# A recurrent attention and gated feed-forward kernel: state products in attention's tiling, and a new plan of the instruction order

## The chip, the cores and the metric

The kernel runs on one core of one Trainium2 chip. The metric is the device time of one execution in microseconds; the time of a kernel is the median of its runs. Five engines work side by side: TensorE (PE; its weight loads are shown as PEld), VectorE (DVE), ScalarE (ACT), GpSimd (POOL) and SyncE (SP), which here issues the DMAs.

## The reference

Three stages follow one another on a batch of 4, 8 heads, 768 tokens, 48 values a head, in float32. `_attn_ref` is a linear recurrence with decay w and a bonus u for the current token; its output, 384 wide, goes into a gated layer with a product over the tokens, and that into a convolution gate.

```python
def _attn_ref(r, k, v, w, u):
    for t in range(S):
        kt, vt, rt = (k[:, :, t], v[:, :, t], r[:, :, t])
        cur = np.einsum('bhd,bhe->bhde', u[None] * kt, vt)
        y[:, :, t] = np.einsum('bhd,bhde->bhe', rt, state + cur)
        state = w[None, :, :, None] * state + np.einsum('bhd,bhe->bhde', kt, vt)

def _moe_ref(x, w_in, w_spatial, b_spatial, w_out):
    h = np.maximum(x @ w_in, 0.0)
    u, v = (h[..., :d_ff // 2], h[..., d_ff // 2:])
    v_n = (v - mu) / np.sqrt(var + 1e-06)
    v_s = np.einsum('ts,bsd->btd', w_spatial, v_n) + b_spatial[None, :, None]
    return ((u * v_s) @ w_out)

def _moe2_ref(x, w_val, conv_w, w_out):
    for k in range(K):
        gate_pre += conv_w[k][None, None, :] * xp[:, k:k + S, :]
    gate = 1.0 / (1.0 + np.exp(-gate_pre))
    return (gate * (x @ w_val) @ w_out)
```

## The kernel before

**Attention in chunks.** A batch is cut into 6 chunks of 128 tokens; the 8 heads lie as 4 pairs, the two heads of a pair at partitions 0 and 64. For chunk i, `load_chunk` brings kT and rT (heads on partitions, two DMAs for rT) and tok (tokens on partitions: k, r, and v in blocks of 32). `prep_chunk` scales them on GpSimd with tables of powers of w, multiplies r, k and u for the bonus, and scales k for the state by the far table (`k_far`, tile tk3); VectorE sums the bonus and ScalarE spreads it on the diagonal of A (L522). `scores` (L545) makes 8 products of 48 rows, and VectorE copies what lies above the diagonal into A (L549). `attend` adds rT times the state S_bd (L573, chunks 1 to 5) and A times v (L577), all in tiles of 32 columns. `state_update` (L606) multiplies k by v into the bank P, 8 products of 48 columns, two column tiles of 64; VectorE scales S_bd by the decay (L612) and adds P (L619; L621 copies in a batch's first chunk). The last chunk of a batch has no state step, so there are 20 in all. All of these products are float32, and each leaves two MATMUL records in the trace.

**Feed-forward part.** float32 values are split into a high and a low part of a faster format, and a product is three MATMULs (`split3`, L632). In order: `value` (pv, 9 products of 512 columns, once a chunk), `gate_in` (pu), `spatial` (ps, L719), `proj` (pd), the convolution on VectorE (L767), `val` (pf), `out_mm` (pg, L804) and the store. The weights come as 64-bit floats; `split_f64` decodes them on ScalarE (L358) and VectorE (L360, L362, L364) and splits them (L401, L402). w_in has two halves of three slices of 512 KB: wv for `value` and wu for `gate_in`.

**The order.** No loop order is kept. Each step is an `op` of the class `Plan` with an engine, an assumed duration, its reads and writes and the buffers that it takes. `Plan.order` simulates the engines and, at each step, takes among the ops that can start earliest the one of highest level: the longest path to the end, plus a bias from the table `FAVOR` (by name, and by chunk, weight slice or stage: stages 0 to 3 are batch 0, 4 the middle batches, 5 the last). A PE op in the tiling of the op before it (`mode`) gets `STAY` more; one in another costs `SWITCH` more time. The modes are "" (full array), "r" (scores), "c" (attend) and "s" (state). Loads are issued by SyncE in that order; a load under 4 KB is assumed to land 1.7 us after its issue, a larger one to share 360 B/ns. The three feed-forward inputs that are single rows (u, and b_sp twice) are spread over the partitions by a TensorE product (L444) and copied by ScalarE (L447). In the planned gaps of the first 40 us, `warm` puts dummy products (L310) before the next op that takes a PSUM buffer.

Of the kernel before, what the change touches and what calls it, by code (L numbers as in the profile page):

```python
# [16 lines left out]
B, H, S, D = 4, 8, 768, 48  # L17
# [19 lines left out]

STAGES = 6
FAVOR = {
    ("attend", 4): 1761900, ("attend", 5): 649800,  # L40
    ("bonus_fill", 'c5'): -99500, ("bonus_fill", 3): -1684500, ("bonus_fill", 4): -306700, ("bonus_fill", 5): -2300,
    ("bonus_sum", 'c3'): -51200, ("bonus_sum", 4): -127800,
    ("bonus_u", 4): 42200, ("bonus_u", 5): -636500,
    ("conv_tap", 3): 230200, ("conv_tap", 4): 204100, ("conv_tap", 5): -665000,
    ("decode_shift", 'wu0'): -635700, ("decode_shift", 'wv2'): 524400,
    ("gate_in", 2): -390500,
    ("k_far", 3): 74400,
    ("k_scale", 3): -1024300,
    ("load_kT", 'c0'): 7800,
    ("load_rT", 'c0'): -340400, ("load_rT", 3): 141900, ("load_rT", 5): -610300,  # L50
    ("load_tok", 'c1'): -1066400, ("load_tok", 4): -17900,
    ("load_wu", 'w1'): 12100,
    ("load_wv", 'w1'): -1258600,
    ("norm_aggr", 'c4'): -134100,
    ("out_copy", 4): 204600,
    ("proj", 3): -35700, ("proj", 5): -12300,
    ("proj_low", 4): -188700,
    ("scores_keep", 4): 272400, ("scores_keep", 5): 278300,
    ("spatial", 4): 685200, ("spatial", 5): -5400,
    ("spatial_high", 3): 258700,  # L60
    ("state", 4): 703000,
    ("val", 3): -36600, ("val", 4): -172300, ("val", 5): -506100,
    ("val_gate", 3): 549700,
    ("val_low", 3): 627700,
    ("value", 4): 558600,
    ("value_relu", 4): 1075200,
    ("x_high", 4): -699900,
    ("x_low", 'c0'): 321000,
}


class Plan:
# [5 lines left out]

    AFTER = {"PE": 200, "ACT": 140, "DVE": 130, "POOL": 100, "SP": 10}
    EVAC = 4000  # L80
    SWITCH, STAY = 95, 408100
    COLD, RAMP = 6900, 40000
    FLOW = 4000
    FIRST = {"SP": 800, "DVE": 900, "ACT": 2150, "POOL": 1900, "PE": 1100}

    def __init__(self):
# [34 lines left out]
    def order(self, slots, free_tags):  # L121
        n = len(self.ops)
        after = lambda a, b: 0 if a == b == "PE" else self.AFTER[a]
        succ = [[] for _ in range(n)]
        for i, o in enumerate(self.ops):
            for p in o[3]:
                succ[p].append((i, after(self.ops[p][0], o[0])))
        left = [len(o[3]) for o in self.ops]
        level = [0.0] * n
        for i in range(n - 1, -1, -1):  # L130
            o = self.ops[i]
            d = o[1] + (2050 + o[6] / 360 if o[6] else 0)
            level[i] = d + max((level[j] + x for j, x in succ[i]), default=0)
        level = [x + o[5] for x, o in zip(level, self.ops)]
        ready = [0.0] * n
        avail = {}
        for i in range(n):
            if not left[i]:
                avail.setdefault(self.ops[i][0], set()).add(i)
        start, end, slot_free = [None] * n, [None] * n, [0.0] * n  # L140
        engine, dma_free, issue_free = dict(self.FIRST), self.FLOW, 0.0
        turn = {t: 0 for t in slots}
        uleft = {k: len(u) for k, u in self.users.items()}
        ufree = {k: 0.0 for k in self.users}
        free = {t: [0.0] * c for t, c in slots.items()}
        dual = {"DVE": (0.0, 0.0), "POOL": (0.0, 0.0)}
        other = {"DVE": "POOL", "POOL": "DVE"}
        mode = ""

        def slot_time(i):  # L150
            t, want = 0.0, {}
            for k in self.ops[i][4]:
                tag = self.tile_tag[k]
                q = want.get(tag, 0)
                want[tag] = q + 1
                if tag not in free_tags and self.tag_order[tag][turn[tag] + q] != k:
                    return None
                if len(free[tag]) <= q:
                    return None
                t = max(t, sorted(free[tag])[q])  # L160
            return t

        for _ in range(n):
            best, first = None, None
            for e, group in avail.items():
                seen = []
                for i in group:
                    t = max(ready[i], engine[e])
                    if self.ops[i][4]:
                        s = slot_time(i)  # L170
                        if s is None:
                            continue
                        t = max(t, s)
                    if self.ops[i][8]:
                        lo, hi = dual[other[e]]
                        if lo <= t < hi:
                            t = hi
                    seen.append((t, i))
                if seen:
                    t = min(seen)[0]  # L180
                    if first is None or t < first or (t == first and e == "POOL"):
                        first, best = t, (e, seen)
            if best is None:
                raise RuntimeError("no order")
            e, seen = best
            i = -max((level[i] + self.STAY * (e == "PE" and self.ops[i][9] == mode), -i)
                     for t, i in seen if t <= first)[1]
            t, o = first, self.ops[i]
            avail[e].discard(i)
            d = o[1]  # L190
            if e == "PE":
                d += self.SWITCH * (o[9] != mode)
                mode = o[9]
            if o[8]:
                dual[e] = (t, t + d)
            start[i], slot_free[i] = t, slot_time(i)
            engine[e] = t + d
            end[i] = t + d
            if o[6]:
                issue_free = max(issue_free, t) + 450 * o[7]  # L200
                if o[6] < 4096:
                    end[i] = issue_free + 1700
                else:
                    dma_free = max(dma_free, issue_free + 850) + o[6] / 360
                    end[i] = dma_free + 900
            for k in o[4]:
                tag = self.tile_tag[k]
                free[tag].remove(min(free[tag]))
                turn[tag] += 1
            for k in self.touch[i]:  # L210
                uleft[k] -= 1
                ufree[k] = max(ufree[k], end[i] + self.AFTER[e])
                if not uleft[k]:
                    free[self.tile_tag[k]].append(ufree[k])
            for j, x in succ[i]:
                ready[j] = max(ready[j], end[i] + x)
                left[j] -= 1
                if not left[j]:
                    avail.setdefault(self.ops[j][0], set()).add(j)
        self.start, self.end, self.slot_free = start, end, slot_free  # L220
        return sorted(range(n), key=lambda i: (start[i], i))

    def run(self, slots, free_tags, keep_clock=None):
# [6 lines left out]
        for i in self.order(slots, free_tags):  # L230
            if self.ops[i][0] == "PE" and keep_clock and self.start[i] < self.RAMP:
                busy = max(busy, self.slot_free[i] + 300)
                cold = max(0.0, min(self.start[i], self.COLD) - busy)
                keep_clock[0] = int(cold // 107 + max(0.0, self.start[i] - max(busy, self.COLD)) // 70)
                busy = self.end[i]
            self.ops[i][2]()
            if keep_clock:
                keep_clock[0] = 0
# [19 lines left out]
def rwkv_mlp_kernel(  # L258
# [59 lines left out]
    def op(*a, **k):  # L318
        plan.op(*a, **k)
# [273 lines left out]
    def state_update(i):  # L593
# [6 lines left out]
        def mm():  # L600
            make()
            k, v = st[tk], vals(i)
            for q in range(NP):
                for g in range(2):
                    h = 2 * q + g
                    nc.tensor.matmul(st[pk][64 * g:64 * g + D, q, :], k[:, D * h:D * h + D],  # L606
                                     v[:, q].rearrange("p (x c) -> p x c", c=Q)[:, g::2], start=True, stop=True)
        op("state", "PE", 520, mm, ((tk, "k"), (tk, "v")), ((pk,),), (pk,), mode="s")
        blocks = S_bd.rearrange("r p (x c) -> r p x c", c=Q)

        def scale():
# [123 lines left out]
    def proj(b, hf, m):  # L735
# [7 lines left out]
        def mm():  # L743
# [2 lines left out]
                for make in mk:  # L746
                    make()
            split3(st[pk], wo, [st[gh], st[gl]], 4, lambda w, kt: w[:, kt, C * m:C * m + C], lambda x, kt: x[:, kt, :])
        op("proj", "PE", ns_r(HALF, 12), mm, tuple((k, q) for k in (gh, gl) for q in range(4)) + wkeys("wo", 4), ((pk,),), (pk, xh, xl, gt) if m == 0 else (pk,))

        def hi():
            nc.scalar.copy(st[xh][:, m, :], st[pk])
# [385 lines left out]
```

## Time and profile before

| | |
|---|---|
| median of 3 runs | 457.17 us (455.93 to 461.05) |
| the profiled execution | 459.84 us |
| its span, first to last instruction | 458.1 us |
| mean granted TensorE clock | 0.989 of full |
| TensorE busy | 434.8 us, 95% of the span |
| VectorE, ScalarE, GpSimd busy | 294.3, 242.9, 154.1 us |

The trace is that of the profiled execution, so its rows add up to 458.1 us and not to the median. Busy time counts overlapping instructions once. MATMUL records overlap one another: a record's length is not what it adds to the stream, and the distance between two starts is read for that. "PE L606 p_bank<-tok 128*48" is a product of line 606 with 128 rows and 48 columns of weights, from tile tok into p_bank.

### The profile page before, as it was taken

The page shows a single profiled execution, that of the slowest core. Times are in us where ns is not written, and L with a number is a line of the kernel's source. Part 1 is how long each engine was busy: PE and PEld are TensorE (multiplying, and loading weights), DVE is VectorE, ACT ScalarE, POOL GpSimd, SP SyncE. Part 2 cuts the span into 40 slices and gives each one's busy share as a digit, 9 for nine tenths or more (in the row PEclk, how much of TensorE's full clock was granted, in tenths as well). Part 3 has the DMA queues.
Part 4 walks back from the last instruction along what each step waited for, and adds up shares of the span by engine and source line. Part 5 has one row for each costly group of instructions (what it writes and reads, how often), then busy time and mean ns, then how long its engine had stood idle before and what let it go on. Part 6 is the DMA issues. An engine that isn't in the chain of part 4 may idle for free.

```text
span 458.1 us, 9861 instructions
## 1 busy us (share of the span) xinstructions
PE 434.8 (95%) x3917; PEld 396.0 (86%) x3917; DVE 294.3 (64%) x599; ACT 242.9 (53%) x575; POOL 154.1 (34%) x179
## 2 busy tenths in 40 slices
PE   5978998899999999999999998999999999999994
PEld 3766887899888889999898797999898889999994
DVE  3388998988987754226977663234986772135860
ACT  1555887566837659225437566433545674334631
POOL 6368752017136675000236658000127630000000
PEclk9979999999999999999999999999999999999998
DMA  8733557542042542000242532000133500000102
GB/s 251 233 113 99 174 172 220 154 133 86 20 124 87 181 124 68 1 18 1 67 126 83 194 115 79 0 18 1 41 114 109 188 4 0 0 19 0 36 14 98
DMA packets 16556, 40.85 MB, mean 89 GB/s; under 512 B 2547, under 2 KB 5622, under 8 KB 16502
## 3 DMA queue, kind: packets, MB, share of 16 engines
q1 hardware_dynamic: 16502, 40.14, 27.9%
q8 instruction: 33, 0.54, 0.5%
q14 instruction: 21, 0.17, 0.1%
HBM read 35.41 MB, written 4.72 MB: 88 GB/s over the span
## 4 chain that ended last, share of the span: by engine, by line
PE 69%; DVE 5%; ACT 4%; DMA 1%; issue 1%; POOL 1%; SPq 0%; ACTq 0%; DVEq 0%; POOLq 0%
PE ps L719 21%; PE pd L632 9%; PE pg L804 8%; PE pu L632 7%; PE pf L632 7%; PE pv L632 6%; PE sc L545 4%; PE y L577 3%; PE y L573 2%; PE p_bank L606 2%; DVE pd L767 2%; DMA tok<-tok 1%; ACT A L522 1%; DVE x2l L761 1%; ACT vh L677 0%
## 5 line engine op out<-in xcount | busy, mean ns | idle before, releaser
L522 ACT ACTIVATE A<-ident,dg 128x128 f32<-128x128 f32 x188 | 58.6, 395 | 17.2 <-DVE dg L512 17.2
L719 PE MATMUL ps<-w_sp_l,vh 128*128 128x384 f32 x192 | 64.9, 338 | 1.3 <-ACT ps L708 1.2
L719 PE MATMUL ps<-w_sp_h,vh 128*128 128x384 f32 x192 | 64.6, 336 | 0.0
L719 PE MATMUL ps<-w_sp_h,vl 128*128 128x384 f32 x192 | 64.5, 336 | 0.0
L767 DVE SCALAR_TENSOR_TENSOR pd<-x,cw,pd 128x384 f32<-128x384 f32 x96 | 56.1, 617 | 4.5 <-ACT pd L764 3.8
L726 DVE TENSOR_TENSOR ps<-ps,u 128x384 f32<-128x384 f32 x32 | 17.5, 566 | 60.9 <-PE ps L719 60.9
L759 POOL COPY x<-x 128x4 f32<-128x4 f32 x12 | 2.2, 186 | 137.4 <-DVE pd L767 137.4
L731 ACT CAST gh<-ps 128x384 fp32r<-128x384 f32 x32 | 15.4, 480 | 52.3 <-DVE ps L726 51.9
L500 POOL TENSOR_TENSOR kT<-kT,tab 112x512 f32<-112x512 f32 x23 | 29.5, 1285 | 32.4 <-DVE dp L360 18.1
L549 DVE COPY_PREDICATED A<-mask,sc 128x512 f32<-128x512 int32 x48 | 34.1, 735 | 7.9 <-ACT A L522 7.0
L504 POOL TENSOR_TENSOR tok<-tok 128x384 f32<-128x384 f32 x24 | 24.2, 1010 | 43.6 <-DMA tok<-tok 34.0
L500 POOL TENSOR_TENSOR rT<-rT,tab 112x512 f32<-112x512 f32 x24 | 31.5, 1316 | 21.7 <-DMA rT<-rT 21.7
L719 PEld LDWEIGHTS ps<-w_sp_l,vh 128*128 128x128 f32 x192 | 36.1, 188 | 2.1 <-ACT ps L708 1.9
L719 PEld LDWEIGHTS ps<-w_sp_h,vl 128*128 128x128 f32 x192 | 36.1, 188 | 0.0
L719 PEld LDWEIGHTS ps<-w_sp_h,vh 128*128 128x128 f32 x192 | 36.1, 188 | 0.0
L632 PE MATMUL pu<-xl,w_in_u_h 128*128 128x384 f32 x96 | 33.4, 348 | 1.1 <-ACT u L696 1.1
L577 PE MATMUL y<-A,tok 128*32 128x128 f32 x768 | 33.8, 279 | 0.0
L632 PE MATMUL pd<-gl,w_out_h 128*128 128x384 f32 x96 | 32.8, 341 | 0.7 <-ACT gate L770 0.7
L632 PE MATMUL pd<-gh,w_out_l 128*128 128x384 f32 x96 | 32.4, 337 | 0.0
L632 PE MATMUL pd<-gh,w_out_h 128*128 128x384 f32 x96 | 32.4, 337 | 0.0
L632 PE MATMUL pu<-xh,w_in_u_h 128*128 128x384 f32 x96 | 32.3, 336 | 0.0
L632 PE MATMUL pu<-xh,w_in_u_l 128*128 128x384 f32 x96 | 32.3, 336 | 0.0
(128 smaller groups left out, 1103.8 us busy)
## 6 DMA issues: line engine op xcount, KB each, us to landing
tok<-tok SPq DMA_DIRECT2D x24, 640.0 KB, 4.3
kT<-kT SPq DMA_DIRECT2D x24, 224.0 KB, 2.6
rT<-rT SPq DMA_DIRECT2D x48, 96.0 KB, 3.4
o<-o SPq DMA_DIRECT2D x24, 192.0 KB, 2.6
raw<-w_in SPq DMA_DIRECT2D x6, 512.0 KB, 6.7
raw<-w_out SPq DMA_DIRECT2D x7, 384.0 KB, 3.8
ws<-w_spT SPq DMA_DIRECT2D x6, 384.0 KB, 4.4
raw<-w_val SPq DMA_DIRECT2D x3, 384.0 KB, 3.1
```

The source lines that it names most:

```text
L500: op(name, e, ns(n), lambda: v.tensor_tensor(a(), a(), b, op=ALU.mult), r, w, dual=True)
L504: op("bonus_rk", e, ns(DM), lambda v=v: v.tensor_tensor(rr(), rr(), kk(), op=ALU.mult), ((tk, "r"), (tk, "k")), ((tk, "r"),), dual=True)
L522: nc.scalar.activation(st[ak][:, p, :], ident, AF.Copy, scale=st[dk][:, 2 * p + g:2 * p + g + 1])
L545: nc.tensor.matmul(st[sk][:, g, p, :], st[kT][rows, p, :], st[rT][rows, p, :], start=True, stop=True)
L549: op("scores_keep", "DVE", 622, lambda g=g, ak=ak: nc.vector.copy_predicated(st[ak], mask.bitcast(I32)[:, None, :].to_broadcast([128, NP, ...
L577: nc.tensor.matmul(y[Q * p:Q * p + Q, j, :], v[:, p, Q * part:Q * part + Q], st["A", i, part % 2][:, p, :], start=(c == 0 and part < 3), s ...
L632: nc.tensor.matmul(ps, wsel(ws[a], kt), xsel(xs[b], kt), start=(i == 0), stop=(i == 3 * n - 1))
L719: nc.tensor.matmul(st[pk], vs[a][:, c % 3, C * j:C * j + C], wsp[w][:, c, ts], start=False, stop=(c == NC - 1 and a == 0 and w == 0), skip ...
L726: op("spatial_gate", "DVE", ns_dve(HALF), lambda: nc.vector.tensor_tensor(st[pk], st[pk], st[uk][:, j, :], op=ALU.mult), ((pk,), (uk, j)), ...
L731: op(wk + "_high", "ACT", ns_act(HALF), lambda: nc.scalar.copy(st[gh][:, j, :], st[gk]), ((gk,),), ((gh, j),))
L767: op("conv_tap", "DVE", 525, lambda k=k: nc.vector.scalar_tensor_tensor(st[pk], tap(k), cw[:, m, k:k + 1], st[pk], op0=ALU.mult, op1=ALU.a ...
L804: nc.tensor.matmul(st[pk], (st[vh], st[vl])[a][:, kt, tt:tt + C], wo2[w][:, kt, :], start=(kt == 0 and w == 1), stop=(kt == KT - 1 and a = ...
```

## The change

The state step's 8 products of 48 columns become 16, of 32 and 16 columns, which go to the four column tiles of 32 that attention uses; its op has the mode "c" and an assumed 500 ns. In the planner, a change between two tilings costs 110 ns and one from or to the full array 165; `STAY` doubles to 826400; all loads, small ones too, share one flow of 330 B/ns in the order of issue, starting at 3.2 us for loads over 4 KB, and a load is not issued before the eighth one back has landed; dummy products are put only into planned gaps over 600 ns; proj's assumed time is a little longer. The table `FAVOR` is replaced. The instructions other than the state products stay as they are in number and shape (but for the dummy products); their order is the plan's.

```diff
-    ("attend", 4): 1761900, ("attend", 5): 649800,
...
-    ("state", 4): 703000,
...
+    ("attend", 4): 835900, ("attend", 5): 1489900,
...
+    ("load_kT", 'c1'): -930700,
+    ("load_rT", 'c0'): 136900, ("load_rT", 'c1'): -792700, ("load_rT", 'c3'): 495000, ("load_rT", 4): -339800, ("load_rT", 5): 494600,
+    ("load_row", 0): 555600,
+    ("load_tok", 'c0'): 407100, ("load_tok", 'c1'): -400200,
+    ("load_wu", 'w1'): 1552200, ("load_wu", 'w2'): 67300,
+    ("load_wv", 'w1'): -1980400,
...
+    ("state", 5): -734900,
...
-    SWITCH, STAY = 95, 408100
+    SWITCH, LEAVE, STAY = 110, 165, 826400
     COLD, RAMP = 6900, 40000
-    FLOW = 4000
+    FLOW, RATE, FLIGHT = 3200, 330, 8
...
-                d += self.SWITCH * (o[9] != mode)
+                if o[9] != mode:
+                    d += self.SWITCH if o[9] and mode else self.LEAVE
                 mode = o[9]
...
-                issue_free = max(issue_free, t) + 450 * o[7]
-                if o[6] < 4096:
-                    end[i] = issue_free + 1700
-                else:
-                    dma_free = max(dma_free, issue_free + 850) + o[6] / 360
+                for _ in range(o[7]):
+                    issue_free = max(issue_free, t, landed[-self.FLIGHT]) + 450
+                    dma_free = max(dma_free, issue_free + 850, self.FLOW if o[6] > 4096 else 0) + o[6] / o[7] / self.RATE
                     end[i] = dma_free + 900
+                    landed.append(end[i])
...
-                keep_clock[0] = int(cold // 107 + max(0.0, self.start[i] - max(busy, self.COLD)) // 70)
+                gap = max(0.0, self.start[i] - max(busy, self.COLD))
+                keep_clock[0] = int(cold // 107 + (gap > 600) * gap // 75)
...
             for q in range(NP):
-                for g in range(2):
-                    h = 2 * q + g
-                    nc.tensor.matmul(st[pk][64 * g:64 * g + D, q, :], k[:, D * h:D * h + D],
-                                     v[:, q].rearrange("p (x c) -> p x c", c=Q)[:, g::2], start=True, stop=True)
-        op("state", "PE", 520, mm, ((tk, "k"), (tk, "v")), ((pk,),), (pk,), mode="s")
+                for at, n in ((0, Q), (Q, D - Q)):
+                    for g in range(2):
+                        col = D * (2 * q + g) + at
+                        nc.tensor.matmul(st[pk][64 * g + at:64 * g + at + n, q, :], k[:, col:col + n],
+                                         v[:, q].rearrange("p (x c) -> p x c", c=Q)[:, g::2], start=True, stop=True)
+        op("state", "PE", 500, mm, ((tk, "k"), (tk, "v")), ((pk,),), (pk,), mode="c")
```

## Rows read from the trace of the kernel before

**Rows 1.** The page: busy time by engine, and the chain that ended last.

```profile
PE 434.8 (95%) x3917; PEld 396.0 (86%) x3917; DVE 294.3 (64%) x599; ACT 242.9 (53%) x575; POOL 154.1 (34%) x179
...
PE 69%; DVE 5%; ACT 4%; DMA 1%; issue 1%; POOL 1%; SPq 0%; ACTq 0%; DVEq 0%; POOLq 0%
```

**Rows 2.** Busy time in four stretches: engines with instruction counts, granted clock, DMA share.

```profile
0.00:20.00 20.00, 15.24 (x96) 9.62 (x98) 6.00 (x20) 6.50 (x17) 8.88 (x17) 1.00 0.83 259
20.00:36.00 16.00, 13.19 (x233) 11.92 (x230) 14.16 (x25) 8.85 (x21) 10.05 (x10) 0.79 0.33 105
36.00:84.00 48.00, 42.51 (x476) 36.16 (x474) 42.53 (x92) 33.92 (x77) 26.81 (x26) 1.00 0.56 168
84.00:460.00 376.00, 363.85 (x3122) 338.25 (x3122) 231.63 (x465) 193.68 (x462) 108.37 (x128) 0.99 0.22 69
```

**Rows 3.** Groups of TensorE instructions by line: attention on A, and the state products.

```profile
L577 PE MATMUL y<-A,tok 128*32 128x128 f32 x768 | 33.8, 279 | 0.0
...
L606 PE MATMUL p_bank<-tok 128*48 128x64 f32 x320 | 13.8, 228 | 3.1 <-POOL rT L500 2.3 <-issue 0.9
```

**Rows 4.** Timeline of TensorE around a state step alone: start, length, records.

```profile
149.40 0.34 PE L804 MATMUL pg<-w_out_h,gvh 128*128 128x384 f32 x1
...
150.53 0.34 PE L632 MATMUL pf<-x2h,w_val_l 128*128 128x384 f32 x1
```

**Rows 5.** Timeline of TensorE around scores alone, then around state and scores.

```profile
99.82 0.34 PE L719 MATMUL ps<-w_sp_h,vh 128*128 128x384 f32 x1
...
101.46 0.34 PE L719 MATMUL ps<-w_sp_h,vl 128*128 128x384 f32 x1
...
112.38 0.34 PE L632 MATMUL pd<-gh,w_out_h 128*128 128x384 f32 x1
...
114.60 0.34 PE L632 MATMUL pd<-gh,w_out_l 128*128 128x384 f32 x1
```

**Rows 6.** Timeline of TensorE, narrow windows: first records of a state and an attention.

```profile
158.03 0.32 PE L606 MATMUL p_bank<-tok 128*48 128x64 f32 x4
...
158.03 0.38 PE L606 MATMUL p_bank<-tok 128*48 128x64 f32 x6
...
169.40 0.30 PE L577 MATMUL y<-A,tok 128*32 128x128 f32 x4
...
169.40 0.41 PE L577 MATMUL y<-A,tok 128*32 128x128 f32 x8
```

**Rows 7.** Waits of the first 40 us: total, times, longest.

```profile
DVE dp L360 <- ACT dp L358: 8.4, 2, 5.4
POOL tok L500 <- ACT tk L894: 7.9, 1, 7.9
```

**Rows 8.** Timeline of the first 37 us, chosen lines of all engines.

```profile
4.46 1.10 SPq L440 DMA_DIRECT2D row<-b_sp  x2
4.57 0.69 DVE L869 TENSOR_TENSOR tab<-pow,pow 112x512 f32<-112x512 f32 x1
...
11.42 1.64 PE L444 MATMUL spread<-row,one 1*128 1x384 f32 x2 [2.03 <-DMA row<-b_sp]
...
13.09 0.48 ACT L447 COPY b_bc<-spread 128x384 f32<-128x384 f32 x1 [5.67 <-PE spread L444]
...
13.47 1.27 ACT L883 ACTIVATE ht<-tab,pow 112x128 f32<-112x128 f32 x4
...
14.81 2.34 PE L310 MATMUL y<-ones 128*64 128x128 bf16 x20
...
17.08 1.01 PE L889 MATMUL y<-ident,ht 112*128 112x112 f32 x4
...
36.15 0.51 PE L632 MATMUL pv<-w_in_v_l,xh 128*128 128x512 f32 x1
```

**Rows 9.** State's work on VectorE, tile S_bd, one batch: durations min, median, max.

```profile
L619 DVE TENSOR_TENSOR S_bd<-S_bd,p_bank x8: 399/419/427, 137.4 to 166.1; 48x256 f32<-48x256 f32 x8
L612 DVE TENSOR_TENSOR S_bd<-S_bd,pow x4: 548/1125/1390, 136.2 to 164.1; 112x384 f32<-112x384 f32 x4
```

More of the change, by code (lines that the diff above doesn't have):

```diff
@@ L48 @@
[L48 to L59, printed above, removed]
@@ L60 @@
-    ("spatial_high", 3): 258700,
-    ("state", 4): 703000,
[L62 to L68, printed above, removed]
+    ("attend", 4): 835900, ("attend", 5): 1489900,
+    ("bonus_fill", 'c1'): -499200,
+    ("bonus_sum", 'c1'): -269300,
+    ("bonus_u", 3): 373900, ("bonus_u", 5): -62300,
+    ("conv_tap", 3): -222500, ("conv_tap", 4): 679600,
@@ new lines @@
+    ("decode_low", 'wv0'): 511900,
+    ("gate_in", 2): -3144600, ("gate_in", 5): 3700,
+    ("gate_relu", 3): 44200, ("gate_relu", 4): 931800, ("gate_relu", 5): 454500,
+    ("k_far", 'c3'): 785500, ("k_far", 'c4'): -1034700, ("k_far", 4): 36800,
+    ("k_scale", 'c0'): 471400,
+    ("load_kT", 'c1'): -930700,
+    ("load_rT", 'c0'): 136900, ("load_rT", 'c1'): -792700, ("load_rT", 'c3'): 495000, ("load_rT", 4): -339800, ("load_rT", 5): 494600,
+    ("load_row", 0): 555600,
+    ("load_tok", 'c0'): 407100, ("load_tok", 'c1'): -400200,
@@ new lines @@
+    ("load_wu", 'w1'): 1552200, ("load_wu", 'w2'): 67300,
+    ("load_wv", 'w1'): -1980400,
+    ("norm_rstd", 4): 301200,
+    ("norm_stats", 'c1'): -1168100, ("norm_stats", 5): 120300,
+    ("out", 4): -14500,
+    ("out_copy", 3): 570100,
+    ("proj", 3): -30200, ("proj", 4): -25400, ("proj", 5): -24400,
+    ("proj_low", 4): 30000, ("proj_low", 5): -393300,
+    ("r_scale", 5): -398700,
+    ("scores_keep", 5): -8200,
+    ("spatial", 4): -6700,
+    ("spread_copy", 3): 270200,
+    ("state", 5): -734900,
@@ L69 @@
+    ("val", 3): -8300, ("val", 4): -698900, ("val", 5): -186500,
+    ("val_low", 5): 117900,
+    ("value", 4): 119600, ("value", 5): -7000,
+    ("value_relu", 4): 36300,
+    ("weight_low", 'wu0'): -1683700,
+    ("x_high", 5): 362200,
 }
@@ L131, in order @@
             o = self.ops[i]
-            d = o[1] + (2050 + o[6] / 360 if o[6] else 0)
+            d = o[1] + (2050 + o[6] / self.RATE if o[6] else 0)
             level[i] = d + max((level[j] + x for j, x in succ[i]), default=0)
@@ L140, in order @@
         start, end, slot_free = [None] * n, [None] * n, [0.0] * n
-        engine, dma_free, issue_free = dict(self.FIRST), self.FLOW, 0.0
+        engine, dma_free, issue_free = dict(self.FIRST), 0.0, 0.0
         turn = {t: 0 for t in slots}
@@ L147, in order @@
         other = {"DVE": "POOL", "POOL": "DVE"}
-        mode = ""
+        mode, landed = "", [0.0] * self.FLIGHT
         def slot_time(i):
@@ L748, in mm @@
             split3(st[pk], wo, [st[gh], st[gl]], 4, lambda w, kt: w[:, kt, C * m:C * m + C], lambda x, kt: x[:, kt, :])
-        op("proj", "PE", ns_r(HALF, 12), mm, tuple((k, q) for k in (gh, gl) for q in range(4)) + wkeys("wo", 4), ((pk,),), (pk, xh, xl, gt) if m == 0 else (pk,))
+        op("proj", "PE", ns_r(HALF, 12, 5.5), mm, tuple((k, q) for k in (gh, gl) for q in range(4)) + wkeys("wo", 4), ((pk,),), (pk, xh, xl, gt) if m == 0 else (pk,))
         def hi():
```

7 lines of the change are left out of this document (removed).

## The prediction

> **What bounds the kernel now.** I read the page first. TensorE is busy for 434.8 of 458.1 us and holds 69% of the chain that ended last [rows 1]. A change can then pay in two ways only: by taking time out of TensorE's own stream, or by letting that stream start earlier. The second view cuts the span in four [rows 2]. From 84 us on, TensorE is busy for 363.9 of 376 us: there the stream itself is the limit, and only shorter or fewer instructions count. From 36 to 84 us VectorE (42.5) and TensorE (42.5 of 48) are level. Before 36 us TensorE's busy time is no measure of work: its records there are small tiled products and dummy products, and VectorE is busy for 6.0 us of the first 20. The first product of the feed-forward part starts at 36.15 us [rows 8], so 36 us of 458 go by before the long stream begins. The granted clock over 20 to 36 us is 0.79; with the two levels of 2.4 and 1.2 GHz that is (1 - 0.79) x 16 / 0.5 = 6.7 us at the lower one.
>
> **The state products, term 1.** The state step is 8 products a chunk, 20 chunks, two records each [rows 3]. I price a visit of TensorE to a tiled shape from the start of the last full-array product before it to the start of the second one after it, less two steady steps of 0.174 us. A state step alone takes 150.53 - 149.40 - 0.35 = 0.78 us [rows 4]. Put beside scores it adds less: scores alone is 101.46 - 99.82 = 1.64, scores and state 114.60 - 112.38 = 2.22, so state adds 0.58 [rows 5]. Inside a visit its products flow at two records every 0.06 us: four records span 0.32 us, six 0.38 [rows 6]. The same flow for all 16 is about 8 x 0.056 = 0.45 us. What lies above 0.45 is the price of changing the tiling: 0.33 us when state is alone, 0.13 us when it is one shape among others. I counted the visits on the timeline: 5 of the 20 states stand alone, 15 beside scores or attention.
>
> The change makes a state 16 products of 64 columns in the 32-column tiling of the attention products, so 32 records. What they cost is not in the trace, as nothing there has four column tiles with 64 columns. Low end: four records go at once, as in attention, where four records of 0.28 us each [rows 3] span 0.30 us, so the last starts some 0.02 us behind the first, and the next four follow 0.11 us later (eight span 0.41) [rows 6]. Half the columns then give a step of about 0.055 us for four, as the pairs now take for two: 8 x 0.056 = 0.45 us, the same as before. A gain below that is excluded, because the same columns stream through each column tile. High end: the mean pace of attention's records, 0.11 / 4 = 0.0275 us, is the fastest in the trace; 32 at that pace are 0.88 us, 0.43 more than now. I take the low end, as the 0.02 us in which four records start is four times quicker than that pace.
>
> In the attention tiling, state can share attention's visit with no change of shape. If all 20 do, 5 x 0.33 + 15 x 0.13 = **3.6 us** go. If the plan leaves them apart, none goes. The planner now gives a product of the current shape 826400 instead of 408100, removes state's own bias of 703000 in the middle batches, and sets -734900 in the last: each of these makes state wait for attention's visit. I take the whole 3.6, nearly all of it after 84 us, where nothing hides TensorE's time. The scores alone (1.29 us each) might join attention too; I leave that out.
>
> **The load plan, term 2.** The old planner lets a small load land 1.7 us after its issue, whatever is queued. The trace says otherwise: the two rows of b_sp, 1.5 KB each, are issued from 4.46 us, and TensorE's spread product that needs the first starts at 11.42 [rows 8]. ScalarE stands 5.7 us behind it, until b_bc's copy at 13.09; the far table follows at 13.47, TensorE turns it at 17.08 behind 20 dummy products [rows 8], and GpSimd waits 7.9 us for the copy [rows 7]. VectorE waits 8.4 us in two pieces for decoded weights that ScalarE has not scaled yet [rows 7]. The table that the far step reads was made by VectorE from 4.57 us on [rows 8], so nothing but the order keeps the far table from starting where ScalarE's wait began, 13.09 - 5.67 = 7.4 us. The new planner queues small loads with the large ones and admits eight at a time, so it should put b_sp's spread after the table and the first decode. That is worth between 0 (something else is as late) and 8.4 us (all of VectorE's wait moves forward). What is late next: the weight slices still have to arrive, and the planner's biases set one slice of w_in's value half back by 1980400, with the two that follow it in its ring of buffers, and one of the other half forward by 1552200. VectorE must make three slices of the value half before the first product at 36.15, and it had 14.2 of 16 us busy from 20 to 36 [rows 2], so earlier work is what it needs. I take **5 us**, just under the 5.7 that ScalarE waits, since that wait is the one that the order makes, and I keep 0 and 8.4 for the range.
>
> **Other edits.** The dummy products come only in planned gaps over 600 ns; one group of 20 takes 14.81 to 17.08 now [rows 8], 2.3 us, in front of the table's turn. Fewer of them could save up to that, or lengthen the time at the lower clock: the 6.7 us above cost at most 3.4 us of TensorE's time, and a second such stretch would cost as much. I take zero between -2.3 and +3.4, as the chain of rows 7 runs through ScalarE and VectorE. Every bias of the plan is new, so all orders move. Where TensorE never runs dry an order costs nothing; from 84 to 460 us it was idle for 12.1 us, part of it the last stores, so I allow 3 us each way. The price of 5.5 in proj and the 500 of state are entries of the planner and run nothing.
>
> **Sum.** The profiled execution took 459.84 us, 458.1 of it span; the median of the three runs is 457.17, so 2.7 less. The terms are differences, so they hold against either: 459.8 - 8.6 = 451.2 for the profiled one, and 457.2 - 3.6 - 5.0 = 448.6 against the median. I predict 449.
>
> **Rivals.**
> A. The start gives nothing: GpSimd's chunk preparation or the late value slices hold the first full-array product near 36 us. For it: VectorE was nearly full from 20 us on, and slices were set back. Against it: every engine waits in the first 20 us for the same small row. 457.2 - 3.6 = 453.6; chance 0.17.
>
> B. The narrow products go at the pace of attention's records. Each state then costs 0.43 us more, 20 x 0.43 = 8.6, and the rest is as forecast: 448.6 + 8.6 = 457.2, no change. It speaks for this that no record stream in the trace is faster on average. Against it are the starts 0.02 us apart for four [rows 6]. Chance 0.08. The Trainium skill, "TensorE: Matmul & The Clock Gate", section "Wait — 56ns, not 53.3ns?", says that warm starts of matmuls never come closer than about 25 ns, however small; by that figure the 32 records would take 0.8 us, an estimate from that page, and the sum would stand near 456. Rows 6 disagree with it for products in different column tiles, so it weighs little here.
>
> C, on the slower side. State behind attention lengthens the loop from chunk to chunk. Now the state product is often done before its attention; put behind it, the add into S_bd waits for 0.45 us of products and some 0.2 us of drain (the solo price of 0.33 spans both ends of a visit). The scaling of S_bd (1.1 us) and two adds (0.42 each) stand in the same loop on VectorE [rows 9], and the next attention waits for them. 20 x 0.65 = 13 us if all of it shows: 448.6 + 13 = 461.6; it decides where TensorE has no full-array product left to run meanwhile, and the time is above the old one once 8.6 of the 13 show. For it: a preference of 826400 for staying in shape postpones tiled work in general, so last values of a batch come later. Against it: idle time of TensorE after 84 us is 12 us in all. Chance 0.14, with the time between 458 and 466.
>
> D. The plan doesn't do what it says: states stay in visits of their own, as they come ready before their chunk's attention (those of a batch's first chunks come many microseconds before). Then only the start pays: 452.2, and some of C's risk is gone; chance 0.08.
>
> **How the numbers follow.** Forecast 0.53, A 0.17, B 0.08, C 0.14, D 0.08. Two times of this kernel within 1% (452.6 to 461.7) can't be told apart. The forecast case lies between 457.2 - 3.6 - 8.4 - 2.3 = 443 and 453; nearly all of it, 0.5, is faster by over 1%. D gives half of its 0.08 to faster, A 0.05 of its 0.17. Slower by over 1% is C's upper half and a little of the unknown order, 0.12. That makes 0.59 faster, 0.29 within, 0.12 slower. The range goes from 443, the start's upper bound, to 459, which takes in A, B and D and leaves out most of C.
>
> **What would show it.** In the changed profile: state records named 128 by 32 and 128 by 16, 640 of them, in groups that touch attention's with no gap; a state's share of such a visit near 0.45 us (0.88 is B); the first pv product near 31 us and ScalarE's wait for b_bc's spread gone or moved behind the far table (else A); in the waits, TensorE idle on S_bd or on x_low between batches (C); p_bank groups between two full-array groups (D). I am wrong if the far table was not what held VectorE, or if the new order starves TensorE at one of the three hand-overs between batches.

## The result, and the profile after

The changed kernel takes 445.59 us (444.06 to 447.06, 4 runs) where the kernel before took 457.86 (455.93 to 461.05, 4 runs): a ratio of 0.9725, 95% interval 0.9653 to 0.9797, so 12.3 us or 2.7% faster. In a later set on one chip the ratio was 0.9758 (0.9710 to 0.9806). The forecast was 449, in a range of 443 to 459. The profiled execution of the changed kernel took 447.06 us, 445.4 of it span.

The page, first its busy times, then its chain by engine, to be read against [rows 1]:

```profile
PE 427.1 (96%) x4241; PEld 394.6 (89%) x4241; DVE 291.0 (65%) x599; ACT 244.0 (55%) x575; POOL 154.7 (35%) x179
...
PE 73%; DVE 9%; DMA 7%; POOL 4%; ACT 3%; issue 2%; SPq 1%; POOLq 0%; DVEq 0%; ACTq 0%
```

Busy time in the same four stretches as [rows 2] (the last ends with the span):

```profile
0.00:20.00 20.00, 17.74 (x224) 13.61 (x226) 13.99 (x34) 10.45 (x24) 14.26 (x22) 0.91 0.89 284
20.00:36.00 16.00, 14.18 (x257) 12.10 (x253) 15.07 (x29) 9.32 (x25) 12.34 (x12) 0.89 0.51 144
36.00:84.00 48.00, 45.41 (x466) 40.45 (x463) 42.02 (x91) 34.75 (x77) 18.32 (x19) 1.00 0.53 165
84.00:446.00 362.00, 349.77 (x3304) 328.42 (x3302) 219.93 (x448) 189.50 (x451) 109.82 (x128) 0.99 0.21 69
```

VectorE has 14.0 us of work in the first 20 instead of 6.0, GpSimd 14.3 instead of 8.9. From 84 us on TensorE stands still for 362 - 349.8 = 12.2 us, less 0.6 that the window reaches past the end: 11.6, against 374.1 - 363.9 = 10.2 before. So the end of the kernel is about as full as it was; the start is not the same.

The timeline of the start, chosen lines, to be read against [rows 8]:

```profile
5.13 0.54 SPq L445 DMA_DIRECT2D row<-b_sp  x2
...
6.47 0.68 DVE L875 TENSOR_TENSOR tab<-pow,pow 112x512 f32<-112x512 f32 x1
...
7.18 1.28 ACT L889 ACTIVATE ht<-tab,pow 112x128 f32<-112x128 f32 x4 [0.74 <-DVE tab L875]
...
7.99 0.85 PE L895 MATMUL y<-ident,ht 112*128 112x112 f32 x4
...
12.16 1.55 PE L449 MATMUL spread<-row,one 1*128 1x384 f32 x4
...
13.11 0.48 ACT L452 COPY b_bc<-spread 128x384 f32<-128x384 f32 x1
...
28.57 0.50 PE L638 MATMUL pv<-w_in_v_l,xh 128*128 128x512 f32 x1
```

The loads of b_sp's rows go out near 5 us as before, but their spreads (12.16) and copies (13.11) now stand behind the far table (7.18 instead of 13.47) and its turn (7.99 instead of 17.08). The first value product comes at 28.57 instead of 36.15. VectorE's wait for scaled weights, 8.4 us in [rows 7], has shrunk to:

```profile
DVE dp L365 <- ACT dp L363: 1.5, 2, 1.3
```

One row tells where the gain lies: the spatial products, with first and last start, of the kernel before and then of the changed one, and after each the busy times from the first of them to the end.

```profile
L719 PE MATMUL ps<-w_sp_l,vh x192: 332/336/448, 76.4 to 415.0; 128*128 128x384 f32 x192
```

```profile
76.40:458.10 381.70, 370.25 (x3159) 344.34 (x3157) 237.96 (x479) 198.78 (x473) 109.55 (x129) 1.00 0.23 71
```

```profile
L725 PE MATMUL ps<-w_sp_l,vh x192: 332/336/442, 64.3 to 402.3; 128*128 128x384 f32 x192
```

```profile
64.30:445.40 381.10, 368.31 (x3409) 346.45 (x3407) 237.62 (x484) 200.81 (x474) 112.35 (x130) 0.99 0.22 73
```

The first spatial product comes 76.4 - 64.3 = 12.1 us earlier. All of batch 0's attention and all 6 value products lie ahead of it in both; of gate_in's products 5 instead of 6 do (45 records instead of 54 by my count), which is 9 x 0.174 = 1.6 us put off to later. So the start gives 10.5 us. From there on it is 381.7 us before and 381.1 after: 0.6 saved, though 1.6 more had to be done.

The state's groups, to be read against [rows 3], and one visit of the new kind (columns as in [rows 4]):

```profile
L612 PE MATMUL p_bank<-tok 128*32 128x64 f32 x320 | 12.6, 220 | 1.0 <-POOL tok L505 1.0
L612 PE MATMUL p_bank<-tok 128*16 128x64 f32 x320 | 12.5, 220 | 0.0
```

```profile
151.62 0.40 PE L638 MATMUL pv<-w_in_v_h,xh 128*128 128x512 f32 x1
...
153.07 0.62 PE L582 MATMUL y<-A,tok 128*32 128x128 f32 x16
153.50 0.63 PE L612 MATMUL p_bank<-tok 128*32 128x64 f32 x32
154.07 1.16 PE L550 MATMUL sc<-rT,kT 48*128 48x128 f32 x16
...
155.44 0.34 PE L638 MATMUL pu<-xh,w_in_u_l 128*128 128x384 f32 x1
```

32 records take 0.63 us from the first start to the last end, at 0.22 each, so 31 starts lie within 0.41 us, 13 ns apart; from the state's first record to that of scores it is 154.07 - 153.50 = 0.57 us. I counted the visits to tiled shapes from the first spatial product on: 34 before, 25 after. Priced as in the prediction, and without the waits inside them, they add up to 63.4 us before and 59.9 after.

### The profile page after: what moved, and what is told of

Same layout as the page of the kernel before. It is cut to its first block, busy times and chain, and to the rows that moved or that the text cites. A ratio compares the mean times of both kernels' runs of the same rounds, so it can differ in the third digit from the quotient of the medians.

```text
span 445.4 us, 10503 instructions
## 1 busy us (share of the span) xinstructions
PE 427.1 (96%) x4241; PEld 394.6 (89%) x4241; DVE 291.0 (65%) x599; ACT 244.0 (55%) x575; POOL 154.7 (35%) x179
## 4 chain that ended last, share of the span: by engine, by line
PE 73%; DVE 9%; DMA 7%; POOL 4%; ACT 3%; issue 2%; SPq 1%; POOLq 0%; DVEq 0%; ACTq 0%
PE ps L725 20%; PE pu L638 10%; PE pd L638 9%; PE pv L638 8%; PE pg L810 7%; PE pf L638 7%; DMA tok<-tok 6%; PE sc L550 4%; PE y L582 4%; PE y L578 2%; PE p_bank L612 2%; POOL tok L505 1%; DVE pd L773 1%; ACT A L527 1%; DVE A L554 1%
```

## Experiments

Each experiment changes one thing, but for two that say so. Where an order is moved by hand, `moved` rearranges the planned list just before it is written out, and each op keeps the dummy products that the plan gave it unless the text says otherwise.

**The narrow products in the old order.** Sixteen products of 32 and 16 columns in the kernel before; the planner still thinks of mode "s" and 520 ns, so the order is the old one.

```diff
-                for g in range(2):
-                    h = 2 * q + g
-                    nc.tensor.matmul(st[pk][64 * g:64 * g + D, q, :], k[:, D * h:D * h + D],
+                for at, n in ((0, Q), (Q, D - Q)):
+                    for g in range(2):
+                        col = D * (2 * q + g) + at
+                        nc.tensor.matmul(st[pk][64 * g + at:64 * g + at + n, q, :], k[:, col:col + n],
```

> The kernel before with its order untouched, and only the state's 8 products of 48 columns cut into 16 of 32 and 16. Theory (four column tiles run side by side, a state costs 0.45 us of flow either way): each state's group keeps its length, about 0.59 us from its first record to the next product when alone, and the total stays within 1 us of before; two or three states that stand right behind or in front of attention lose a change of tiling, 0.1 us each. Rival (narrow products start no faster than attention's records, 0.0275 us apart): a state grows by 0.43 us, the total by 6 to 9 us.

Measured: 457.46 us, 0.9959 of before (0.9931 to 0.9987). Its state groups:

```profile
L607 PE MATMUL p_bank<-tok 128*32 128x64 f32 x320 | 13.2, 226 | 0.0
L607 PE MATMUL p_bank<-tok 128*16 128x64 f32 x320 | 12.9, 225 | 0.0
```

Twice the records, no longer each. By the same price as in the prediction, the five states that stand alone cost 0.77 to 0.78 us, as before (0.78 to 0.79), and the one visit of state, attention, scores fell from 3.55 to 3.41. Rival B, 8.6 us more, falls. That the total is 1.9 us lower is more than the few merged visits explain; I have no cause for the rest.

**The wide products in the new order.** The reverse, in the changed kernel.

```diff
-                for at, n in ((0, Q), (Q, D - Q)):
...
+                for g in range(2):
+                    h = 2 * q + g
```

> The changed kernel with its order untouched, and only the state's products put back to 8 of 48 columns. Theory: each state that stands beside attention pays a change of tiling again, 0.13 us in some 17 places, 0.33 us where it stood between attention and full-array products: the total grows by 2 to 3.5 us. Rival (the gain after the start comes from the new order alone, the tiling is worth nothing): within 0.5 us of the changed kernel.

Measured: 448.03 us, 0.9737 of before (0.9669 to 0.9806), with no run of the changed kernel in that set. So it was run again beside it.

> The changed kernel as it is, as the measure for the other three of this set on one chip. Expected: 0.965 to 0.980 of before, as in the first comparison.

> The changed kernel with the state's products put back to 8 of 48 columns, order untouched, a second time and beside the changed kernel itself. Theory: 2 to 3.5 us longer than the changed kernel, from changes of tiling beside attention. Rival: within 1 us of it, the tiling being worth nothing once waits are counted.

Measured: the changed kernel 448.77 us, 0.9758 (0.9710 to 0.9806); with wide products 448.59, 0.9744 (0.9701 to 0.9786). The totals don't differ. The visits do; the same visit as above, with wide products:

```profile
151.71 0.40 PE L637 MATMUL pv<-w_in_v_h,xh 128*128 128x512 f32 x1
...
153.16 0.62 PE L582 MATMUL y<-A,tok 128*32 128x128 f32 x16
153.72 0.65 PE L611 MATMUL p_bank<-tok 128*48 128x64 f32 x16
154.30 1.16 PE L550 MATMUL sc<-rT,kT 48*128 48x128 f32 x16
...
155.68 0.34 PE L637 MATMUL pu<-xh,w_in_u_l 128*128 128x384 f32 x1
```

From the last product before to the second after it is 155.68 - 151.71 = 3.97 us here and 155.44 - 151.62 = 3.82 with narrow ones, 0.15 us for the change of tiling. The difference sits where attention ends: from its last 16 records to state it is 153.72 - 153.16 = 0.56 us with wide products and 153.50 - 153.07 = 0.43 with narrow ones; from state to scores it is 0.58 and 0.57. Over all visits from the first spatial product on, without waits, it is 61.5 us against 59.8. So the tiling saves 1.7 us there, and the total doesn't show it. One thing differs early: in both profiles with wide products the granted clock held its full level from 14 to 28 us, while in both of the changed kernel it fell twice there. The rows are of the changed kernel and of the wide one, for that stretch (busy times by engine, then granted clock, DMA share, GB/s):

```profile
14.00:28.00 14.00, 12.18 (x211) 10.85 (x210) 12.69 (x22) 7.46 (x18) 10.76 (x10) 0.76 0.77 229
```

```profile
14.00:28.00 14.00, 11.52 (x210) 9.35 (x210) 12.98 (x23) 8.17 (x19) 13.00 (x13) 1.00 0.68 219
```

The first value product came at 27.53 and 27.69 us with wide products, at 28.57 and 29.49 in the two profiles of the changed kernel. The two profiles of the later set agree with this account: the first spatial product comes 0.95 us earlier with wide products (64.15 against 65.10), and from there on the kernel takes 1.5 us longer (383.7 against 382.2). Those of the earlier sets do not: there the wide kernel reaches its first spatial product later (66.38 against 64.32). So it is not shown what took the 1.7 us back.

**The row of b_sp, in the old order.** Only the two spreads and copies of b_sp are moved, behind the far table's copy.

```diff
+        rows = [i for i in seq if name(i) in (("spread", 3), ("spread_copy", 3))]
+        rest = [i for i in seq if i not in rows]
+        at = next(n for n, i in enumerate(rest) if name(i)[0] == "table_far_copy") + 1
+        return rest[:at] + rows + rest[at:]
```

> The kernel before in its own order, except that the two spread products of b_sp and their copies stand behind the far table's copy; all loads are issued as before. Theory (the wait for that small row holds the start): the far table starts near 7.5 us instead of 13.5, scores of chunk 0 come near 15 us instead of 22, the first full-array product of value near 30 us instead of 36.15, and the total falls by 4 to 7 us. Rival (what counts is that chunk 0's rT is loaded first, or the order of the weight slices): the first value product stays at 34 to 36 us and the total falls by less than 1.5 us.

Measured: 453.90 us, 0.9890 of before (0.9818 to 0.9961), 5.1 us less by that ratio. Chosen lines of its start:

```profile
7.28 1.28 ACT L897 ACTIVATE ht<-tab,pow 112x128 f32<-112x128 f32 x4
...
9.07 1.01 PE L903 MATMUL y<-ident,ht 112*128 112x112 f32 x4
...
13.62 0.48 ACT L461 COPY b_bc<-spread 128x384 f32<-128x384 f32 x1 [2.96 <-PE spread L458]
...
16.84 0.70 DVE L374 TENSOR_SCALAR dp<-dp 128x512 int32<-128x512 int32 x1 [5.24 <-ACT dp L372]
...
18.38 1.16 PE L559 MATMUL sc<-rT,kT 48*128 48x128 f32 x16
...
31.65 0.19 PEld L646 LDWEIGHTS pv<-w_in_v_l,xh 128*128 128x128 f32 x1
```

The far table comes at 7.28 and the value product at 31.65, 4.5 us earlier. ScalarE met the row again at 13.62, and VectorE's second decode waited behind it until 16.84. Scores came at 18.4, later than expected: between the table's turn and them TensorE ran the two spreads of the row, state 0 and 82 dummy products (10.01 to 18.4). The next run therefore takes the row out of the start altogether, behind the attention of chunk 1, and with it the 23 dummy products that stood ahead of its spreads, so it changes two things:

```diff
-        at = next(n for n, i in enumerate(rest) if name(i)[0] == "table_far_copy") + 1
+        at = next(n for n, i in enumerate(rest) if name(i) == ("attend", "c1")) + 1
...
+                dummies[i] = 0 if self.labels[i] == ("spread", 3) else keep_clock[0]
```

> The kernel before, with b_sp's two spreads and copies taken out of the start altogether (behind the attention of chunk 1) and without the 23 dummy products that stood ahead of them; loads as before. With the row only behind the far table, ScalarE met it again at 13.6 us and VectorE waited 5.2 us for the second decoded slice. Theory (that wait was the next late thing): state 0 comes near 13 us instead of 16.3, the first value product between 27 and 30 us instead of 31.65, and the total is 3 to 4 us below that run. Rival (chunk 0's rT, issued last, or the weight slices now hold the start): first value product stays at 31 to 32 us, total within 1.5 us of that run.

Measured: 451.83 us, 0.9810 of before (0.9760 to 0.9860), 8.7 us less by that ratio and 7.7 by the medians. Its TensorE, and its first spatial product:

```profile
9.21 1.01 PE L903 MATMUL y<-ident,ht 112*128 112x112 f32 x4
...
13.08 0.26 PE L620 MATMUL p_bank<-tok 128*48 128x64 f32 x1
...
15.18 1.16 PE L559 MATMUL sc<-rT,kT 48*128 48x128 f32 x16
...
29.81 0.50 PE L646 MATMUL pv<-w_in_v_l,xh 128*128 128x512 f32 x1
```

```profile
L733 PE MATMUL ps<-w_sp_l,vh x192: 332/336/447, 73.2 to 408.8; 128*128 128x384 f32 x192
```

State 0, scores and the value product are within 1.5 us of the changed kernel's (11.59, 14.27, 28.57), with every load as before. So the order of chunk 0's loads was not what held the first products; the place of the small row was, with the 23 dummy products that stood ahead of its spreads. The lead doesn't all last: the first value product is 6.3 us earlier than before, the first spatial product only 3.1 (73.2 instead of 76.4), where the run before this one had 70.1. What takes it back in between is open.

**The row of b_sp, in the new order.** First with its loads moved too, which is a second change: all six ops of the row stand in front of the far table in the list.

```diff
+        rows = [i for i in seq if name(i) in (("load_row", 3), ("spread", 3), ("spread_copy", 3))]
+        at = next(n for n, i in enumerate(rest) if name(i)[0] == "table_far")
```

> The changed kernel in its own order, except that the loads of b_sp's two rows, their spread products and copies stand ahead of the far table. Theory: ScalarE waits for the row again, the far table moves from 7.2 to near 12 us, the first value product from 28.6 to 32 or later, and the total grows by 3 to 6 us. Rival (the row is not the cause, or lands early enough here): the total stays within 1 us of the changed kernel.

Measured: 463.41 us, 1.0084 of before (1.0040 to 1.0128). The far table's place in the list is behind many loads, so SyncE issued the rows at 16.79 us only, and ScalarE waited for them:

```profile
22.95 0.48 ACT L466 COPY b_bc<-spread 128x384 f32<-128x384 f32 x1 [16.13 <-PE spread L463]
...
24.61 1.28 ACT L903 ACTIVATE ht<-tab,pow 112x128 f32<-112x128 f32 x4
```

A far table 17.4 us later makes the kernel about 15 us slower (463.41 against 448.03 for the wide one of the same set); the late row need not be all of that, as other loads moved up and the granted clock from 14 to 28 us was 0.50. To keep the loads where they were, only spreads and copies were moved:

```diff
-        rows = [i for i in seq if name(i) in (("load_row", 3), ("spread", 3), ("spread_copy", 3))]
+        rows = [i for i in seq if name(i) in (("spread", 3), ("spread_copy", 3))]
```

> The changed kernel with its loads in their own order, and only b_sp's spread products and copies ahead of the far table on TensorE and ScalarE. In the earlier run of this kind the loads had moved too, the far table came at 24.6 us and the whole gain was lost. Theory (a delay of the far table passes to the end nearly whole): the row lands near 11 to 12 us, the far table moves from 7.2 to 12 to 14 us, the first value product from 28.6 to 32 to 35, the total grows by 3 to 6 us. Rival: other work covers such a delay; the total grows by less than 1.5 us.

Measured: 454.78 us, 0.9895 of before (0.9839 to 0.9952), 6.0 us above the changed kernel of the same set. ScalarE, then TensorE's spread:

```profile
7.15 0.48 ACT L466 COPY u_bc<-spread 128x384 f32<-128x384 f32 x1 [1.42 <-PE spread L463]
14.50 0.48 ACT L466 COPY b_bc<-spread 128x384 f32<-128x384 f32 x1 [6.87 <-PE spread L463]
...
16.15 1.28 ACT L903 ACTIVATE ht<-tab,pow 112x128 f32<-112x128 f32 x4
```

```profile
12.85 2.89 PE L463 MATMUL spread<-row,one 1*128 1x384 f32 x4 [5.73 <-DMA row<-b_sp]
```

The rows were issued from 5.45 us and the spread that needs the first began at 12.85, set free by the DMA. About half of the whole gain is gone by this one move.

**The load model alone.** The planner of the kernel before with the new flow for loads; biases, mode prices and products are old.

```diff
-                if o[6] < 4096:
-                    end[i] = issue_free + 1700
-                else:
-                    dma_free = max(dma_free, issue_free + 850) + o[6] / 360
-                    end[i] = dma_free + 900
+                for _ in range(o[7]):
+                    issue_free = max(issue_free, t, landed[-self.FLIGHT]) + 450
+                    dma_free = max(dma_free, issue_free + 850, self.FLOW if o[6] > 4096 else 0) + o[6] / o[7] / self.RATE
+                    end[i] = dma_free + 900
+                    landed.append(end[i])
```

> The kernel before with one part of the change alone: the planner's new load model (one flow for all loads, eight under way); biases, state products and mode prices are the old ones. Its first eleven loads stay in the old order, but b_sp's spreads now stand behind state 0 and the far table in front of u_bc. Theory (the load model's worth is the place of that small row): first value product between 27 and 31 us, the total 5 to 9 us below before. Rival (the gain needs the new biases, chunk 0's rT loaded first above all): first value product after 33 us, the total within 2 us of before.

Measured: 465.97 us, 1.0156 of before (1.0097 to 1.0215): slower. The first value product came at 29.67, where I had expected it, but the total went the other way. The spatial products, and the busy times from the first of them on:

```profile
L718 PE MATMUL ps<-w_sp_l,vh x192: 332/336/522, 70.2 to 420.0; 128*128 128x384 f32 x192
```

```profile
70.20:463.50 393.30, 375.17 (x3168) 348.76 (x3167) 239.35 (x479) 199.79 (x473) 110.66 (x130) 0.99 0.22 69
```

The first spatial product is 6.2 us earlier than before, 1.6 of which are nine gate_in products put off, as in the changed kernel. From there it is 393.3 us instead of 381.7, 10.0 more without those 1.6: TensorE stands still for 18.1 us instead of 11.5 and is busy for 4.9 more. My reading is that the old biases belong to the old list; no run changes the biases alone.

**All but the load model.** The changed kernel with the old model of loads.

> The changed kernel with the old load model put back in the planner, all else new; its first loads keep the new order, and b_sp's spreads stand ahead of the far table again. Theory: like the run with the spreads moved by hand, the far table comes at 12 to 16 us, the first value product at 35 to 38 us, and the total is 5 to 9 us above the changed kernel (453 to 458). Rival (biases and tiling carry the gain): within 2 us of the changed kernel.

Measured: 470.57 us, 1.0225 of before (1.0152 to 1.0297), about 22 us above the changed kernel of the set before, on the same chip. The plan puts b_sp's spreads ahead of the far table's turn, and ScalarE waits for them before it copies the turned table:

```profile
14.24 0.48 ACT L453 COPY b_bc<-spread 128x384 f32<-128x384 f32 x1 [5.09 <-PE spread L450]
...
17.45 0.54 ACT L901 COPY tk<-y 128x192 f32<-128x192 f32 x2 [0.96 <-PE y L896]
```

The value product comes at 34.28, a little ahead of the 35 to 38 that I had expected, but the total is 22 us above the changed kernel where I had expected 5 to 9. The first spatial product comes at 76.7, 12.4 us later than in the changed kernel, though nine gate_in products fewer lie ahead of it (36 records instead of 45). From there to the end another 13.0 are lost, 1.6 of them for those nine:

```profile
76.70:470.80 394.10, 372.75 (x3417) 348.91 (x3415) 242.86 (x483) 201.16 (x475) 111.36 (x130) 0.99 0.22 71
```

394.1 us from the first spatial product on, 21.4 of them without TensorE work.

**The dummy products.** The old rule in the changed kernel, then none at all.

```diff
-                gap = max(0.0, self.start[i] - max(busy, self.COLD))
-                keep_clock[0] = int(cold // 107 + (gap > 600) * gap // 75)
+                keep_clock[0] = int(cold // 107 + max(0.0, self.start[i] - max(busy, self.COLD)) // 70)
```

> The changed kernel with the old rule for dummy products, order untouched. In the changed kernel the granted clock fell twice between 14 and 28 us; with wide state products it stayed up there and the first value product came 1 to 1.8 us earlier. Theory: the small gaps that the new rule leaves unfilled let the clock fall; with the old rule it stays up, the first value product comes near 27.5 us and the total is 1 to 2 us lower. Rival: the few more dummy products change nothing, total within 1 us.

Measured: 448.62 us, 0.9788 of before (0.9740 to 0.9836); the changed kernel was 0.9758. With 168 dummy products instead of 153 the mean granted clock from 14 to 28 us was 0.88 instead of 0.76 and 0.78:

```profile
14.00:28.00 14.00, 12.69 (x232) 10.85 (x231) 12.81 (x23) 7.92 (x19) 11.39 (x11) 0.88 0.70 228
```

The value product came at 27.87, and nothing of it is seen in the total (448.77 for the changed kernel in the set before).

```diff
-                keep_clock[0] = int(cold // 107 + (gap > 600) * gap // 75)
+                keep_clock[0] = 0
```

> The changed kernel with no dummy products at all, order untouched. Theory: the clock stays at its lower level through most of the first 28 us, the small products there take up to twice as long, the first value product comes 2 to 5 us later and the total grows by as much. Rival (the start waits for loads, ScalarE and VectorE, not for TensorE's clock): first value product within 1 us of 28.6 to 29.5, the total within 1 us.

Measured: 450.04 us, 0.9821 of before (0.9773 to 0.9869). Three lines of TensorE:

```profile
15.34 2.08 PE L550 MATMUL sc<-rT,kT 48*128 48x128 f32 x16
...
28.49 1.26 PE L550 MATMUL sc<-rT,kT 48*128 48x128 f32 x16
29.68 0.50 PE L638 MATMUL pv<-w_in_v_l,xh 128*128 128x512 f32 x1
```

The trace records no granted clock before 28.7 us here, but scores at 15.34 take 2.08 us, as at the lower of the two levels (1.26 at 28.49, 1.16 at the full one elsewhere). Even so the value product comes at 29.68, only 0.2 to 1.1 us later than in the two profiles of the changed kernel, and the total is 1.4 us above that of the old rule in the same set, with intervals that overlap. Theory and rival each held in part: products took up to twice as long, and little came of it.

## Why the prediction was right, point by point

**What bounds the kernel** held. After 84 us TensorE leaves about as little idle as before (11.6 us against 10.2; the prediction's 12.1 counted 1.9 us beyond the end of the span), and the gain lies in what comes ahead of its long stream.

**Term 1, the state products, 3.6 us.** The flow of 0.45 us held: 32 records start within 0.41 us, and the unchanged order takes no longer with them. The Trainium skill, "TensorE: Matmul & The Clock Gate", section "Wait — 56ns, not 53.3ns?", has a floor of about 25 ns between starts; here starts in different column tiles lie 13 ns apart, so the floor doesn't hold across tiles. The saving in the visits is 63.4 - 59.9 = 3.5 us, near the 3.6; half of it, 1.7, is the tiling in the new order, the rest comes from fewer visits. But it is not all in the total: TensorE's idle time after 84 us grew by 1.4 us, so that from the first spatial product on 0.6 + 1.6 = 2.2 us are saved, and the pair of runs with narrow and wide products shows no difference. That the tiling shortens the kernel is not shown.

**Term 2, the load plan, 5 us, was mis-sized: the start gave 10.5.** The cause was right and is shown from both sides: taken out of the old order, with 23 dummy products, the row gives 7.7 us; put into the new one it takes 6.0. "5 us, just under the 5.7 that ScalarE waits" was the wrong row to lean on. The wait also held the table's turn and GpSimd's 7.9 us, and VectorE's 8.4 us, which was my upper end, came forward nearly whole: the value product came 7.6 us earlier. The other 2.9 of the 10.5 were gained between the first value and the first spatial product, where TensorE's stretch shortened from 40.2 to 35.7 us (1.6 of that is the work put off). This points to the new order as a whole and not to the row: every kernel with that order and narrow products has 35.6 to 36.5 us there, also with the row put back (35.6); the four with the old order have 38.5 to 43.6, and the two crossed kernels 40.5 and 42.4. The small row's lateness I put down to the queue: with the spreads ahead of the far table, the row was issued from 5.45 behind nine loads and set its spread free at 12.85, while u's row of the same size, issued at 1.75 behind two, was there by 5.47. No run issues the row of b_sp ahead of the large loads, so that is argued. The Trainium skill, "DMA: Bandwidth & Descriptors", section "Queues, rings and completion order", says that a DMA engine takes the descriptors of a ring in order; these times agree.

**"I allow 3 us each way" for the order failed as a bound.** With the load model and the rest of the plan out of step, the part after the first spatial product grew by 10.0 us against the kernel before in one crossed kernel, and by 11.4 against the changed one in the other, the work put off left out. In the changed kernel both belong together, so it didn't show. For the same reason the change can't be told as a sum of its parts: the load model alone is slower, all but the load model is slower, both are 12 us faster. The zero for the dummy products held: the old rule changes nothing in the total.

**The sum** owes something to luck. The start gave 10.5 us, more than the 8.4 that I held possible for it, and the part behind it 2.2 instead of 3.6, so one error hides a part of the other. With all of the 3.6 the time would have stood at the edge of the range, 457.2 - 10.5 - 3.6 = 443.1.

**The rivals.** A (the start gives nothing) and B (narrow products slow) are refuted by the runs above. For A the prediction counted a bias that sets one value slice back by 1980400; the old table already set the same slice back by 1258600. C (state behind attention lengthens the chunk loop): TensorE's waits after the first spatial product name no S_bd, and the time from there on shrank. D: of the 15 states after the first spatial product, 12 share a visit with attention, two stand beside scores and one alone, so D was true for three.

## What to carry to other kernels

Where a list scheduler orders the work, look for the instruction that was placed early because its model thought its input was there: a wait of several engines on one small transfer is the sign, and moving that one op shows its worth before anything is tuned. A start-up delay that all engines share can pass to the end for the most part (here 7.7 us gained and 6.0 lost by moving one row, in the first case with 23 dummy products, where the first value product moved by 6.3 and 8.9), so price it by the longest of the waits behind it and not by the first. That holds while the order behind the start stays as it was: with the load model alone the first value product came 6.5 us earlier and the kernel ended 7 us later. Figures fitted to one cost model are a part of it: the new model alone made the old kernel 7 us slower, and the old model alone made the new kernel 22 us slower.

## What the runs showed of the hardware that was not expected

Sixteen products of 32 and 16 columns flowed in the time of eight of 48: in four column tiles the records of 64-column float32 products start 13 ns apart, where two column tiles took them 28 ns apart. Without dummy products, and with scores that took twice as long in the first 20 us, the kernel lost some 1.4 us of 449, by medians whose intervals overlap: TensorE waited for other engines there (2.5 us for GpSimd ahead of its first state product), and holding its clock up bought little. A change between two tilings cost 0.15 us in the middle of a visit, where a visit of its own cost state 0.33.
